# Moving eight rows of each segment from one softmax to the other in a memory-recurrent attention kernel

## The chip, the cores and the metric

One NeuronCore of one Trainium2 chip runs the whole program. The metric is the device time of one execution in microseconds, the median of several runs. The core's engines work side by side: TensorE (PE, its weight loads listed apart as PEld), VectorE (DVE), ScalarE (ACT), GpSimd (POOL) and the queue that starts the DMA transfers (SP). Each engine runs its own instructions in a fixed order and waits on semaphores for the others.

## The reference: what is computed

2048 tokens of width 512 go through two blocks, each with a layer norm ahead and a residual sum. The first is attention with a memory, cut into 64 segments of 32 tokens that run one after the other; the second is a two-layer perceptron (512 to 1792 to 512, gelu).

```python
for s in range(n_seg):                                  # 64 segments
    h = concatenate([mem, xs], axis=1)                  # 8 memory rows + 32 tokens
    q, k, v = (einsum('btd,dhe->bhte', h, W) for W in (Wq, Wk, Wv))   # 32 heads of 128
    scores = einsum('bhqe,bhke->bhqk', q, k) * scale
    scores = where(mask, scores, -1e9)                  # memory rows see all 40 keys, tokens are causal
    o = einsum('bhqk,bhke->bhqe', softmax(scores), v)
    o = einsum('bhte,hed->btd', o, Wo)
    mem = o[:, :8, :]                                   # memory of the next segment
    outs.append(o[:, 8:, :])
```

Only the eight memory rows pass from one segment to the next. The chain from one memory to the next (projection, scores, softmax, product with the values, output projection) is the sequential part; everything else may be done beside it.

## The kernel before, in words

**Three kinds of rows.** A segment's 40 rows are its 8 memory rows, its first 24 tokens and its last 8 tokens, called late here. The first two kinds make 32 rows, which fill a 32-column tile of TensorE's array: `hT` holds them, and the passes `Q0`, `Q1`, `K0`, `K1`, `V0`, `V1` (16 heads each, four units of four 128x32 matmuls with 512 columns) project them with the segment's order of work. The late rows of four segments (a block) make 32 rows too, `hB`; the passes `F0`, `F1` project them a block ahead, keys in the first segment of a block, queries in the second, values in the third. In the fourth, `F` is the output projection of the late rows of the block before (`wo_B`). The results lie in `QTB`, in a region of `KALL` and in `VBD`.

**Two softmaxes.** `sc_mm` makes the scores of the memory rows and the late rows together (parts `SC0`, `SC1`, 16 heads each). For each head the stationary operand `ZC` has 32 columns: the 8 memory queries and the 8 late queries of this head in the place that belongs to the head, zeros elsewhere, so that two heads share one 32-row strip of the result. The moving operand has 64 columns: the 32 keys of the segment (token and memory) and 32 late keys, of which the head's 8 stand in its place. A half therefore has a score tile of 128 rows x 2 slots x 64 columns. `sc_softmax` takes the maximum over both slots (`nmc`), then for each slot an exponential with its sum (`Ea`, `EC`), a reciprocal (`ra`, `rsc`), and a multiply that also separates even from odd strips (`PCa`, `PC`); one 32x32 transpose of all of it gives `PTC`. `pv_c` (`PV0`, `PV1`) multiplies with the values `VS` and, for late keys, with `VBD`; one evacuation goes to the memory columns of `OT` (`OTm`), and after `PV1` `pv_c_b` evacuates the late rows' part to `OTB`. `qb_fill` copies the late queries of the next segment into `ZC` ahead of time, on GpSimd.

`sa_mm` makes the scores of the 24 token rows (part `SA`): 32 matmuls with 32 columns, eight heads a strip, a tile of 128 rows x 8 x 32. In `QT` the eight memory queries still stand in the last columns, so their scores come out too and are not used. `SA`'s softmax and `sa_tail` (multiply `PA`, transpose `PTA`, four copies to the block-diagonal `BD`) run into the next segment, whose part `PVA` (`pv_a`) multiplies with the values; two evacuations go to `OT` (`OTx0`, `OTx1`).

**What sets the order.** TensorE's order is written out by hand in `ORDERS`, one list for each of the four segments of a block; for the third it runs Q and K passes, `SC0`, V and `F1` units, `SC1`, more V and `F1` units, `PV0`, `PVA`, a unit of `F1`, two units of `WO`, `PV1`, six units of `WO`, `SA`, `F0`. (`WO` is the output projection.) The other engines' orders come from a planner, `schedule` at L235: it places each operation, in the order of due times in `PLAN`, into the earliest gap of its engine, with a duration written beside each operation (`dur`). An operation made with `either` may go to one of several engines; the one that ends it first is taken, VectorE with a handicap of 0.2 (`LEAN`). `HOME` fixes some of them: `PA` and the first copy of memory queries `ZCm0` go to GpSimd.

**Instruction blocks.** `align` (L476) counts TensorE's instructions in blocks of 256. At the start of a segment it sets how many spare weight loads (`pad`, emitted in the passes at L869) bring the segment to a fixed place in its block: `PHASE` is 0, 64, 128, 192 for the four kinds of segment. If it is past that place by no more than `SLIP` (24), none are inserted; past that, the spares fill up to the same place of the next block, at most 8 in a unit (`PADS`). `ni` beside each TensorE operation is its count of instructions.

Lines used below: L871 and L604 are the passes, L1036 `sc_mm`, L1044 to L1063 `sc_softmax`, L1074 and L1079 `pv_c`, L1104 `sa_mm`, L1114 to L1118 its softmax, L1125 `PA`, L1127 `PTA`, L1131 `BD`, L1142 `pv_a`, L1170 the output projection, L1176 the new memory (`hT`), L926 the copy of memory queries into `ZC`, L933 `qb_fill`, L912 the transposes of queries and keys, L889 and L890 evacuations, L1364 a matmul of the perceptron that runs early.

Of the kernel before, what the change touches and what calls it, by code (L numbers as in the profile page):

```python
# [28 lines left out]
HALVES = ("kq", "KA", "QT", "ZCm", "VS", "nmc", "Ea", "EC", "ra", "rsc", "PCa", "PC", "PTC", "OTm", "OTx", "KB", "QTB", "VSB")  # L29
# [5 lines left out]
         57: (("w1", 0, 0.6),), 58: (("hn", 3, 0.2), ("w1", 6, 0.4)), 59: (("w1", 1, 0.1), ("w1", 2, 0.8)), 60: (("w1", 3, 0.2), ("w1", 4, 0.5)), 61: (("w1", 5, 0.1),)}  # L35
# [13 lines left out]
        "Ea0": (4.18,) * 4,  # L49
        "EC0": (4.59,) * 4,  # L50
        "ra0": (4.66,) * 4,
        "PCa0": (4.86,) * 4,
# [11 lines left out]
        "Ea1": (5.51,) * 4,  # L64
        "EC1": (5.92,) * 4,
        "ra1": (5.98,) * 4,
        "PCa1": (6.1,) * 4,
# [6 lines left out]
        "OTB": (8.2, 8.48, 8.24, 8.2),  # L74
        "SAp": (7.37,) * 4,
# [13 lines left out]
        "ZCb": (5.92, 3.35, 3.35, 3.35),  # L89
# [13 lines left out]
         ("B", "Q", 0, (0, 5)), "Q0", ("B", "Q", 0, (1, 4)), "Q1", "Z", "SC0", "SC1", ("B", "Q", 1, (0, 5)), "PV0", "PV1", "SA", "WO", ("T", "WO", 0, 3),  # L103
# [35 lines left out]
class Sched:  # L139
# [419 lines left out]
P = 128  # L559
SEG = 32  # L560
MEM = 8
NA = 24
E = 128
# [4 lines left out]
HP = H // 2  # L568
F = 1792
# [52 lines left out]
def build_kernel(nc, A_x, A_mem0, A_Wq, A_Wk, A_Wv, A_Wo, B_w1, B_b1, B_w2, B_b2, out):  # L622
# [3 lines left out]
    with st:  # L626
# [18 lines left out]
        maskR = sb("maskR", [P, 2, 64])  # L645
        maskA = sb("maskA", [P, 32])
        maskCF = sb("maskCF", [P, P], F32)
        maskAF = sb("maskAF", [P, 32], F32)
# [3 lines left out]
        KALL = sb("KALL", [P, 4 * HP + 1, 32, 2])  # L652
        QTB = sb("QTB", [P, 2, HP, 32, 2])
        QT = sb("QT", [P, HP, 32, 2])
        ZC = sb("ZC", [P, 2, H, 32])
# [3 lines left out]
        nmc = sb("nmc", [P, 2, 2], F32)  # L659
        smc = sb("smc", [P, 2, 2], F32)  # L660
        rsc = sb("rsc", [P, 2, 2], F32)
        EC = sb("EC", [P, 2, 2, 64], F32)
        PC = sb("PC", [P, 2, 2, 64, 2])
        PTC = sb("PTC", [P, 2, 2, 64, 2])
        even = sb("even", [P, 2], F32)
        SA = sb("SA", [P, 8, 32], F32)
# [3 lines left out]
        PA = sb("PA", [P, 4, 32, 2])  # L670
        PTA = sb("PTA", [P, 4, 32, 2])
        BD = sb("BD", [P, 2, 4, 4, NA, 2])
# [27 lines left out]
        def sc_place(bank):  # L700

            w = quad[:, bank, 0:128] if bank < 4 else ps[bank][:, 0:128]
            return w.rearrange("p (a n) -> p a n", a=2), ("ps", bank)
# [23 lines left out]
        mL = maskL[:].rearrange("p (a b) -> p a b", a=2)  # L727
        for hl in range(2):
            S.op("pool", lambda e, hl=hl: e.affine_select(mL[:, hl, 8:16], mL[:, hl, 8:16], pattern=[[1, 8]], compare_op=ALU.not_equal, fill=1.0,
                                                          base=8 * hl, channel_multiplier=-1), reads=["maskL"], writes=["maskL"])  # L730
            S.op("pool", lambda e, hl=hl: e.affine_select(mL[:, hl, :], mL[:, hl, :], pattern=[[0, 16]], compare_op=ALU.not_equal, fill=1.0,
                                                          base=-16 - hl, channel_multiplier=1), reads=["maskL"], writes=["maskL"])

        S.op("pool", lambda e: e.memset(maskR[:], 0.0), writes=["maskR"])
        for sl in range(2):
            for i in range(4):
                v = maskR[:, sl, 32 + 8 * i:40 + 8 * i]
                for hl in range(2):
                    if i == 2 * sl + hl:
                        if hl == 0:  # L740

# [647 lines left out]
        for s in range(NS):  # L1389
# [46 lines left out]
            def tail(s):  # L1436
# [15 lines left out]
                if 0 < s < NS - 1:  # L1452
                    qb_fill(s + 1, [S.last_writer[("KA", s % 2, 0)]])
# [233 lines left out]
```

## Time and profile before

| what | value |
|---|---|
| time, median of 3 runs | 819.95 us (818.89 to 820.13) |
| span of the profiled execution | 817.0 us (the profile gives no other time of this execution) |
| TensorE busy | 780.8 us, 96% |
| VectorE, ScalarE, GpSimd busy | 622.1, 529.6, 351.2 us |
| first segment's Q pass to the last segment's `SA` | 31.8 us to 711.3 us of the span |

The 64 segments take most of the span; ahead of them the weights are loaded, behind them the perceptron runs. Three cautions for reading: a matmul's end is modelled and overlaps the next one's start, so distances between starts say more than busy time; a row of the order of time can stand for many instructions in a row (x16); and a wait for several semaphores is put down to one of them.

### The profile page before, as it was taken

What the parts mean: (1) busy time and instruction counts of PE and PEld (TensorE: products, weight loads), DVE (VectorE), ACT (ScalarE), POOL (GpSimd) and SP (SyncE); (2) the same over time, 40 slices, a digit from 0 to 9 for tenths busy, and PEclk for the clock granted to TensorE, in tenths of its full rate; (3) what the DMA queues carried; (4) which work ended last, traced back from release to release, by engine and by line L of the source; (5) the groups of instructions that cost most, each with busy time, mean ns of one, the idle gap of its engine ahead of it and who ended that gap; (6) DMA issues with size and microseconds to landing.
All of it is one profiled execution on the core that took longest, in us unless ns stands there. A gap on an engine that the chain in (4) does not pass through costs nothing.

```text
span 817.0 us, 43604 instructions
## 1 busy us (share of the span) xinstructions
PE 780.8 (96%) x19317; PEld 426.6 (52%) x18878; DVE 622.1 (76%) x2008; ACT 529.6 (65%) x1522; POOL 351.2 (43%) x886
## 2 busy tenths in 40 slices
PE   3788999999999999999999999999999999999998
PEld 1345555555556555555555556555555555544443
DVE  3268797989898989898989898888899887833211
ACT  2446677767776767777777777767676766643442
POOL 5023334545454545454545454545463535367200
PEclk9989999999999999999999999999999999999999
DMA  8950010111101010101010201010112131265200
GB/s 341 391 173 16 4 25 15 30 30 27 32 21 39 17 42 14 45 10 43 10 49 10 49 10 49 10 49 3 49 29 62 37 91 26 76 173 147 55 26 26
DMA packets 65449, 48.03 MB, mean 59 GB/s; under 512 B 29028, under 2 KB 61676, under 8 KB 65260
## 3 DMA queue, kind: packets, MB, share of 16 engines
q1 hardware_dynamic: 64928, 44.98, 18.5%
q8 instruction: 150, 2.46, 1.3%
q14 instruction: 39, 0.32, 0.1%
q10 hardware_dynamic: 332, 0.27, 0.1%
HBM read 31.08 MB, written 8.13 MB: 48 GB/s over the span
## 4 chain that ended last, share of the span: by engine, by line
PE 77%; DVE 8%; ACT 7%; SPq 5%; issue 1%; DMA 1%; DVEq 0%
PE ps L871 33%; PE ps L1170 15%; PE quad L1576 6%; PE ps L604 5%; PE ps L1569 5%; ACT EC L1053 4%; PE quad L1074 4%; ACT kq L889 3%; DVE KALL L912 3%; SPq L791 2%; PE ps L1209 2%; DVE PC L1061 2%; SPq L774 2%; PE ps L1104 2%; DVE nmc L1044 2%; PE quad L1142 2%
## 5 line engine op out<-in xcount | busy, mean ns | idle before, releaser
L871 PE MATMUL ps<-WQ,hT 128*32 128x512 bf16 x2048 | 159.9, 384 | 5.7 <-DVE hT L1176 5.6
L1170 PE MATMUL ps<-WO,OT 128*32 128x256 bf16 x4224 | 141.3, 274 | 1.4 <-DMA WO<-in_A_Wo_dram 0.9
L871 PE MATMUL ps<-WV,hT 128*32 128x512 bf16 x1780 | 142.5, 379 | 0.0
L890 ACT ACTIVATE kq<-ps 128x512 bf16<-128x512 f32 x146 | 87.2, 597 | 66.1 <-PE ps L871 65.8
L1125 POOL TENSOR_TENSOR PA<-SA,rsa 128x256 bf16<-128x256 f32 x64 | 39.8, 621 | 187.4 <-DVE rsa L1118 174.5
L889 ACT CAST kq<-ps 128x512 bf16<-128x512 f32 x160 | 93.4, 583 | 37.8 <-PE ps L871 37.8
L1170 PEld LDWEIGHTS ps<-WO,OT 128*32 128x32 bf16 x4224 | 96.4, 96 | 24.4 <-issue 2.9
L1131 POOL COPY BD<-PTA 32x192 bf16<-32x192 bf16 x256 | 96.4, 376 | 16.7 <-DVE PTA L1127 0.9
L1061 DVE SCALAR_TENSOR_TENSOR PC<-EC,rsc,even 128x128 bf16<-128x128 f32 x256 | 94.6, 371 | 6.6
L871 PE MATMUL ps<-WK,hT 128*32 128x512 bf16 x1292 | 93.6, 379 | 0.0
L871 PEld LDWEIGHTS ps<-WQ,hT 128*32 128x32 bf16 x2048 | 60.5, 96 | 59.8 <-issue 19.4
L912 DVE STREAM_TRANSPOSE KALL<-kq 128x256 f32<-128x256 f32 x160 | 70.5, 441 | 22.9 <-ACT kq L889 20.6
L1053 ACT ACTIVATE EC<-quad,nmc 128x64 f32<-128x64 f32 x252 | 77.1, 311 | 7.6 <-DVE nmc L1044 0.9
L604 PE MATMUL ps<-WK,hT 128*32 128x512 bf16 x756 | 76.5, 382 | 0.0
L889 ACT CAST VS<-ps 128x512 bf16<-128x512 f32 x126 | 73.8, 586 | 0.9
L889 ACT CAST OT<-quad 128x128 bf16<-128x128 f32 (+1 forms) x193 | 65.2, 358 | 10.7 <-PE quad L1079 7.7
L912 DVE STREAM_TRANSPOSE QT<-kq 128x256 f32<-128x256 f32 x128 | 57.0, 446 | 18.7 <-ACT kq L890 18.6
L871 PEld LDWEIGHTS ps<-WV,hT 128*32 128x32 bf16 x1780 | 51.9, 96 | 33.7 <-issue 1.4
L1572 ACT ACTIVATE WQ<-ps,b1t 128x512 bf16<-128x512 f32 x42 | 28.9, 688 | 51.9 <-PE ps L1569 51.9
L1116 ACT ACTIVATE SA<-SA 128x256 f32<-128x256 f32 x64 | 26.7, 417 | 55.0 <-DVE SA L1115 52.7
L871 PEld LDWEIGHTS ps<-WK,hT 128*32 128x32 bf16 x1292 | 38.5, 97 | 44.5 <-issue 19.6
L1222 POOL TENSOR_TENSOR opT<-TTB,TTS 32x64 bf16<-32x64 f32 x128 | 40.3, 315 | 32.4 <-DVE opT L1176 23.2
(160 smaller groups left out, 1485.9 us busy)
## 6 DMA issues: line engine op xcount, KB each, us to landing
WV<-in_A_Wv_dram SPq DMA_DIRECT2D x4, 1024.0 KB, 10.4
WK<-in_A_Wk_dram SPq DMA_DIRECT2D x4, 1024.0 KB, 18.0
WQ<-in_A_Wq_dram SPq DMA_DIRECT2D x4, 1024.0 KB, 18.9
WO<-in_A_Wo_dram SPq DMA_DIRECT2D x16, 256.0 KB, 7.8
v_last<-VSB SPq DMA_DIRECT2D x60, 64.0 KB, 3.1
VBD<-v_last SPq DMA_DIRECT2D x60, 64.0 KB, 2.9
h_mid<-xr SPq DMA_DIRECT2D x16, 128.0 KB, 1.9
WQ<-h_mid SPq DMA_DIRECT2D x4, 512.0 KB, 4.3
```

Of the source, the lines that this page charges most:

```text
L604: return e.add_instruction(mybir.InstMatmult(name="I-%d" % (4000000 + _kept[0]), engine=mybir.EngineType.PE, start_tensor_calc=start, stop ...
L871: ins = e.matmul(o, l, m, start=(k == 0), stop=(k == DC - 1), tile_position=(0, 32 * j), skip_group_check=True)
L889: return {"act": (lambda e: e.copy(out, src), t_act(n, ps_)), "dve": (lambda e: e.tensor_copy(out, src), 0.155 + 1.0e-3 * n * fast)}
L890: return {"act": (lambda e: e.mul(out, src, scale_), t_act(n, ps_)), "dve": (lambda e: e.tensor_scalar(out, src, scale_, None, ALU.mult), ...
L912: S.op("dve", lambda e: e.transpose(out, src), reads=[("kq", i)], writes=[key], dur=t_dve(256) + 0.02)
L1053: return e.activation(EC[:, r, sl, :], o[:, sl, :], ACTF.Exp, bias=nmc[:, r, sl:sl + 1], accum_out=smc[:, r, sl:sl + 1])
L1061: S.op("dve", lambda e, sl=sl, xc=xc: e.scalar_tensor_tensor(PC[:, r, :, :, sl], xc, rsc[:, r, sl:sl + 1], ev, ALU.mult, ALU.mult), reads= ...
L1131: S.narrow(S.op("pool", lambda e, j=j, rows=rows: e.tensor_copy(BD[rows, par, :, j, :, :], PTA[rows, :, 0:NA, :]), reads=["PTA"], writes=[ ...
L1170: ins = e.matmul(ps[bank][32 * j:32 * j + 32, 0:256], lhs(slot(h)), wo_cols(h, b), start=(k == 0), stop=(k == 15), tile_position=(0, 32 * ...
L1222: return e.tensor_tensor(o[32 * q:32 * q + 32, c:c + 2], x, y, ALU.add)
L1569: ins = e.matmul(ps[bank][:, 0:SBT], W1[:, cc, fc * P:(fc + 1) * P], hnT_of(k)[:, cc, :], start=(cc == 0), stop=(cc == DC - 1))
L1576: S.op("pe", lambda e: e.matmul(quad[:, t, :], gT_of(k, fc)[:, t * P:(t + 1) * P], W2[:, fc, :], start=(fc == 0), stop=(fc == FC - 1)), re ...
```

## The change

The late queries and the late keys leave the memory rows' softmax and join the token rows'.

- `ZC` holds memory queries alone. Four heads (before: two) share a 32-row strip, so a half has one slot of 64 columns: one maximum, one exponential, one reciprocal, one multiply, a transpose of half the size. `ZC` has one buffer instead of two; `qb_fill` goes. Matmuls of `sc_mm` keep their number and size.
- In `QT`, once the memory queries have been copied out, `ql_fill` puts the segment's 8 late queries in their place; `kl_fill` puts the 8 late keys behind the segment's 32 keys in `KALL`, whose rows become 40 wide. Both may go to ACT, VectorE or GpSimd, and both stand ahead of `SA`. `sa_mm`'s 32 matmuls have 40 columns instead of 32, the softmax 8x40 columns instead of 8x32.
- `sa_tail` gets a second multiply (`PL`, 64 columns, VectorE or GpSimd) ahead of the transpose, which is 160 words wide instead of 128, and a masked copy `BDL` of the late keys' probabilities (VectorE or GpSimd). `BD` keeps all 32 rows' columns.
- `pv_c` has 16 instead of 32 columns in its eight matmuls, 64 instead of 128 in its two. `pv_a` has 64 instead of 48 columns in its sixteen, and four more with 64 columns for the late keys. `OTB` is evacuated after `PVA`, a segment later.
- The masks are rebuilt to match, planner durations and due times are set anew, and one early load of the perceptron's weights moves a segment later.

```diff
-        "Ea0": (4.18,) * 4,
-        "ra0": (4.66,) * 4,
-        "PCa0": (4.86,) * 4,
+        "QL": (7.0,) * 4,
+        "KL": (6.5,) * 4,
+        "PL": (12.86,) * 4,
+        "BDL": (15.6,) * 4,
...
-        return HOP[p.eng]
+        return HOP[p.eng] + (0.06 if o.eng == "pe" else 0.0)
...
+        def ql_fill(s):
+            bk, sg = s // 4, s % 4
+            dst, src = words(QT[:])[:, :, NA:SEG], words(QTB[:, bk % 2])[:, :, 8 * sg:8 * sg + 8]
+            S.either({"act": (lambda e: e.copy(dst, src), 0.34), "dve": (lambda e: e.tensor_copy(dst, src), 0.24), "pool": (lambda e: e.tensor_copy(dst, src), 0.34)},
+                     reads=[("QTB", bk % 2, q) for q in range(2)], writes=[("QL", 0), ("QT", 0), ("QT", 1)])
+
+        def kl_fill(s):
+            bk, sg = s // 4, s % 4
+            dst, src = k_words(s % 2)[:, :, 32:LK], k_words(bk % 2, True)[:, :, 8 * sg:8 * sg + 8]
...
                     for j in range(4):
                         h = 16 * r + 4 * j + i
...
-                        sl = i // 2
-                        ins = e.matmul(o[32 * j:32 * j + 32, sl, :], ZC[:, par, h, :], rhs, start=False, stop=(i == 3),
+                        ins = e.matmul(o[32 * j:32 * j + 32, :], zc_window(h), rhs, start=False, stop=(i == 3),
                                        tile_position=(0, 32 * j), skip_group_check=True)
...
         def sc_softmax(s, r, bank):
-            for sl, names in enumerate((("Ea", "sa", "ra", "PCa"), ("EC", "smc", "rsc", "PC"))):
+            S.op("act", lambda e: e.activation(EC[:, r, :], o, ACTF.Exp, bias=nmc[:, r:r + 1], accum_out=smc[:, r:r + 1]),
+            S.op("dve", lambda e: e.reciprocal(rsc[:, r:r + 1], smc[:, r:r + 1]), reads=[("smc", r)], writes=[("rsc", r)], dur=0.16)
+            S.op("dve", lambda e: e.scalar_tensor_tensor(PC[:, r].rearrange("p k b -> p b k"), xc, rsc[:, r:r + 1], ev, ALU.mult, ALU.mult),
...
         def sa_tail(s):
+            S.either({k: ((lambda e: e.tensor_tensor(PA[:, 4].rearrange("p (i u) r -> p r i u", i=4), SA[:, :, SEG:LK].rearrange("p (r i) u -> p r i u", r=2), bcl, ALU.mult)), w)
+                      for k, w in (("dve", 0.24), ("pool", 0.32))}, ["SA", "rsa"], ["PL"], after=after)
...
-                S.narrow(S.op("pool", lambda e, j=j, rows=rows: e.tensor_copy(BD[rows, par, :, j, :, :], PTA[rows, :, 0:NA, :]), ...
+                S.narrow(S.op("pool", lambda e, j=j, rows=rows: e.tensor_copy(words(BD[rows, par, :, j, :, :]), words(PTA[rows, 0:4])), ...
+            S.either({k: ((lambda e: e.tensor_tensor(BDL[:, par], src, msk, ALU.mult)), w) for k, w in (("dve", 0.3), ("pool", 0.45))},
+                     reads=["PTA", "maskD"], writes=[("BDL", par)])
...
         def pv_a(s):
+                for r in range(2):
+                    for t in range(2):
+                        rows = slice(64 * t, 64 * t + 64)
+                        o = quad[:, 2 + t, 256 * r:256 * r + 256].rearrange("p (n q) -> p n q", q=32)[:, :, NA:SEG]
+                        ins = e.matmul(o, VBD[rows, bk % 2, sg, r, :], BDL[rows, s % 2, r], start=False, stop=True, tile_position=(64 * t, 0), skip_group_check=True)
-                 writes=AQ, dur=0.29, mode=MH, ni=32)
+                 writes=AQ, dur=0.27, mode=MH, ni=40)
...
                 elif name == "SA":
+                    ql_fill(s)
+                    kl_fill(s)
                     sa_mm(s, bank_of[name])
```

More of the change, by code (lines that the diff above doesn't have):

```diff
@@ L28 @@
 PAUSES, PAUSE_IN, PAUSE_US = 3, 64, 0.5
[L29 removed]
+HALVES = ("kq", "KA", "QT", "ZCm", "VS", "nmc", "EC", "rsc", "PC", "PTC", "OTm", "OTx", "KB", "QTB", "VSB")
 BONUS = {}
@@ L562 @@
 NA = 24
+LK = 40
 E = 128
@@ L1145, in pv_a @@
-            S.op("pe", f, reads=[("VS", par, 0), ("VS", par, 1)] + [("BD", s % 2, j) for j in range(4)], writes=AQ, dur=0.29, mode=MH, ni=32)
+                        c0 = 256 * (k // 4) + 32 * (k % 4)
+                        o = quad[:, 2 + t, c0:c0 + 160].rearrange("p (b q) -> p b q", q=32)[:, 0:5:4]
+                        e.matmul(o, VS[rows, par, k // 4, (k % 4) * E:(k % 4 + 1) * E], BD[rows, s % 2, k // 2, 2 * t:2 * t + 2, :, k % 2],
+                                 start=(k == 0), stop=False, tile_position=(64 * t, 0), skip_group_check=True)
```

246 lines of the change are left out of this document (110 added, 136 removed).

## The prediction, made before the change was built

> **What bounds the kernel now.** I read the page first, then busy time by stretch, then the order of time of one steady segment, TensorE first and the engines that feed it after.
>
> ```profile
> span 817.0 us, 43604 instructions
> PE 780.8 (96%) x19317; PEld 426.6 (52%) x18878; DVE 622.1 (76%) x2008; ACT 529.6 (65%) x1522; POOL 351.2 (43%) x886
> ```
>
> ```profile
> 376.24:387.31 11.07, 10.40 (x296) 5.76 (x284) 9.33 (x32) 7.42 (x22) 5.42 (x13) 1.00 0.02 3
> 387.31:397.73 10.42, 10.37 (x296) 5.82 (x277) 9.00 (x31) 7.73 (x24) 4.79 (x13) 1.00 0.06 17
> 397.73:408.04 10.31, 10.28 (x297) 5.73 (x285) 9.66 (x33) 7.50 (x22) 5.66 (x15) 1.00 0.02 5
> 408.04:418.35 10.31, 10.28 (x297) 5.71 (x286) 9.10 (x31) 7.51 (x23) 4.47 (x12) 1.00 0.37 93
> ```
>
> These are four consecutive segments (one block) at full clock: TensorE is the only engine without room, so the loop is worth what TensorE's start times say. A busy PE can still wait, since a matmul's 0.40 us tail covers short gaps; I therefore read distances between starts, here in the third segment.
>
> ```profile
> 401.19 0.30 PE L1036 MATMUL quad<-KALL,ZC 128*32 128x64 bf16 x16
> ...
> 403.19 0.61 PE L871 MATMUL ps<-WV,hT 128*32 128x512 bf16 x8
> 403.62 0.40 PE L871 MATMUL ps<-WV,hB 128*32 128x512 bf16 x4
> 404.05 0.27 PE L1074 MATMUL quad<-PTC,VS 64*128 64x32 bf16 x8
> 404.14 0.23 PE L1079 MATMUL quad<-PTC,VBD 64*128 64x128 bf16 x2
> 404.20 0.37 PE L1142 MATMUL quad<-BD,VS 64*128 64x48 bf16 x16
> 404.51 0.40 PE L871 MATMUL ps<-WV,hB 128*32 128x512 bf16 x4
> 404.73 0.62 PE L1170 MATMUL ps<-WO,OT 128*32 128x256 bf16 x16
> 405.29 0.27 PE L1074 MATMUL quad<-PTC,VS 64*128 64x32 bf16 x8
> 405.40 0.22 PE L1079 MATMUL quad<-PTC,VBD 64*128 64x128 bf16 x2
> 405.55 1.50 PE L1170 MATMUL ps<-WO,OT 128*32 128x256 bf16 x48
> ```
>
> Eight matmuls of 512 columns take 0.43 (403.19 to 403.62), so four take 0.215. The four at 403.62 hold the engine until 403.835, yet the first PV of the memory rows (PV0) starts at 404.05: 0.215 lost. What it waits for is in VectorE's order:
>
> ```profile
> 402.56 0.39 DVE L1061 SCALAR_TENSOR_TENSOR PC<-EC,rsc,even 128x128 bf16<-128x128 f32 x1
> 402.86 0.15 DVE L1058 RECIPROCAL rsc<-smc 128x1 f32<-128x1 f32 x1
> 402.99 0.29 DVE L1044 TENSOR_REDUCE nmc<-quad 128x2 f32<-128x128 f32 x1
> 403.20 0.35 DVE L1061 SCALAR_TENSOR_TENSOR PC<-EC,rsc,even 128x128 bf16<-128x128 f32 x1
> 403.59 0.31 DVE L1063 STREAM_TRANSPOSE PTC<-PC 128x128 f32<-128x128 f32 x1
> ```
>
> PTC lands at 403.90 and PV0 starts 0.15 later. Not all of the 0.215 is that wait, because the array changes its tiling there (128x32 to 64x128). A late segment shows the change alone:
>
> ```profile
> 686.54 0.39 PE L1364 MATMUL ps<-xr,hT 128*128 128x512 bf16 x1
> 686.87 0.27 PE L1074 MATMUL quad<-PTC,VS 64*128 64x32 bf16 x8
> ```
> ```profile
> 686.19 0.31 DVE L1063 STREAM_TRANSPOSE PTC<-PC 128x128 f32<-128x128 f32 x1
> ```
>
> There PTC was ready at 686.50, and from one 512-column matmul (0.215) to PV0 still 0.33 pass: the change costs 0.33 - 0.215 = 0.115. So the removable wait at PV0 is about 0.10 to 0.11 a segment. At PV1, 0.56 from the start of 16 matmuls whose work is 0.44 (48 take 1.32, below in the same order as at 405.55) leaves 0.12, the change alone.
>
> **The change part by part.** *Memory softmax.* Each half loses one exponential with its accumulator read, one reciprocal and one L1061 multiply, and its transpose and maximum halve. Before PV0 the second multiply (403.20) and the interposed second reciprocal go. From 402.56 the chain is one multiply (0.39) and a transpose below 0.31, so PTC is ready near 403.3 instead of 403.90. That is before 403.835, and the wait is gone: 58 steady segments x 0.11 = **-6.4 us**. Bounds: 0 if the wait is all tiling change, -7 if all 0.12 beyond it go.
>
> In the three first looping segments no late-token pass fills TensorE, and the same chain stands bare:
>
> ```profile
> 78.43 0.83 PE L871 MATMUL ps<-WV,hT 128*32 128x512 bf16 x12
> 79.73 0.27 PE L1074 MATMUL quad<-PTC,VS 64*128 64x32 bf16 x8 [0.46 <-ACT EC L1053]
> ```
>
> 12 matmuls take 0.645 and the tiling change 0.115, so 1.30 - 0.76 = 0.54 is wait. The chain shortens by about 0.6, so I take 0.5 x 3 = **-1.5 us** (0 to -1.6). The first segment's gain is lost: its output projection waits for weights. In the segments after 680 the hT wait follows, PV0 has none.
>
> *PV matmuls.* PV0 and PV1 keep their count at half the columns. Two of 128 columns took 0.06 (404.14 to 404.20), so with 64 about 0.03: -0.03 each. PVA gains four matmuls and its 16 go from 48 to 64 columns. The row's eight 32-column ones took 0.09 to 0.11, 0.0125 each, which I read as a load bound; 16 in 0.31 less the tiling change are 0.0125 each as well, with 48 columns. 64 columns stream in the time of half of 128, so they fit nearly. Four more cost 0.05. Net -0.06 + 0.05 + 0.02 = 0.01, x 61 = **+0.6 us** (0 to +4).
>
> By the Trainium skill, "TensorE: Matmul & The Clock Gate", section Back-to-back issue gap, matmuls of 1 to 64 columns all cost about the 25 ns issue floor. It agrees that the wider 16 cost nothing; at its price the four would be 0.1 us, the term +3.7 and the time 3.1 us later. The rows' 0.0125 (two row groups side by side) decide.
>
> *Token softmax, 256 to 320 columns.*
>
> ```profile
> L1044 DVE TENSOR_REDUCE nmc<-quad 128x2 f32<-128x128 f32 x126 | 36.8, 292 | 0.6 <-PE quad L1036 0.6
> L1114 DVE TENSOR_REDUCE nma<-ps 128x8 f32<-128x256 f32 x64 | 27.2, 425 | 2.9 <-PE ps L1104 0.9
> L1222 POOL TENSOR_TENSOR opT<-TTB,TTS 32x64 bf16<-32x64 f32 x128 | 40.3, 315 | 32.4 <-DVE opT L1176 23.2
> ```
>
> 128 more elements cost 0.133, so 64 cost 0.067 on each of three VectorE steps; the exponential gets about 0.035. The probabilities PA start 0.235 later. The new small multiply (PL, 64 elements) is near 0.3 on GpSimd by the last row, or 0.2 on VectorE. Behind PA on GpSimd stands the copy of the memory queries (ZC) that the scores SC0 need:
>
> ```profile
> 399.98 0.62 POOL L1125 TENSOR_TENSOR PA<-SA,rsa 128x256 bf16<-128x256 f32 x1 [2.57 <-DVE rsa L1118]
> 400.62 0.29 POOL L926 COPY ZC<-QT 128x128 bf16<-128x128 bf16 x1
> ```
> ```profile
> 389.29 0.62 POOL L1125 TENSOR_TENSOR PA<-SA,rsa 128x256 bf16<-128x256 f32 x1 [2.29 <-DVE rsa L1118]
> 390.19 0.29 POOL L926 COPY ZC<-QT 128x128 bf16<-128x128 bf16 x1 [0.28 <-DVE QT L912]
> ```
>
> In the third segment the copy follows PA at once; in the second it has 0.28 to spare. SC0 starts at 401.19, the copy ends at 400.91: with 0.15 for the signal (as at PV0) the slack is 0.13. So PA alone pushes SC0 by 0.235 - 0.13 = 0.1 in segments like the third, by nothing in those like the second; PL adds up to 0.3 where it is queued on GpSimd ahead of the copy, and little on VectorE, in the gap before QT. From 0 to 0.33 a segment; I take 0.05, near the second segment's slack: 58 x 0.05 = **+2.9 us** (0 to +19).
>
> *Cover.* The copies of late queries and keys into QT and KALL may run any time from the memory queries' copy (400.91) to the output projection's end (near 407.0), behind which the token scores SA stand; ACT (7.5 of 10.3) and GpSimd (5.7) have room. If put in VectorE's queue ahead of KALL they would cost TensorE their 0.3. The masked copy BDL needs only PTA (401.2) and is wanted at PVA; late it would cost up to its 0.3. OTB's evacuation goes to after PVA, the same size. The wait of the next Q for hT stays: its chain and its filling work do not change. The masks' fewer GpSimd steps lie under the weight load.
>
> *Instruction stream.* PVA adds four matmuls and four weight loads to each segment. The kernel fills segments up to a fixed place in 256-instruction blocks with spare weight loads (L869):
>
> ```profile
> L869 PEld LDWEIGHTS <-hT x16: 92/92/93, 376.2 to 418.3; 128*32 128x32 bf16 x16
> ```
> ```profile
> 385.66 0.24 PE L1104 MATMUL ps<-KALL,QT 128*32 128x32 bf16 x12
> 386.54 0.30 PE L1104 MATMUL ps<-KALL,QT 128*32 128x32 bf16 x20 [0.64 <-issue]
> ```
> ```profile
> q8 instruction: 150, 2.46, 1.3%
> ```
>
> Four spares a segment exist, eight instructions come: each segment overruns by about four. By the code, after some six segments (slip over 24) about 230 spares are inserted, some ten times. A block is one packet (38,195 TensorE instructions / 150 = 255), and where it comes late, the token scores stand for 0.64, as here in a first segment of a block. I take +1.0 us (0: the spares ride under matmuls; +9: 0.3 in 16 first segments and 0.4 at ten refills).
>
> The Trainium skill, "Runtime: NRT & Kernel Launch", section Instruction fetch mechanics, has 16 KiB blocks fetched ahead, the crossing mostly hidden; by it the term is 0 and the time 1.0 us earlier. The row with 0.64 shows a crossing that is not.
>
> **The sum.** -6.4 - 1.5 + 0.6 + 2.9 + 1.0 = -3.4 us. The profile gives the span, 817.0; the median of 819.95 lies 2.95 above, which I leave as it is around the span: 819.95 - 3.4 = **816.5 us**.
>
> **Rivals.**
> *The copy behind PA (slower).* One mechanism at one place: GpSimd takes PL ahead of ZC in every second segment kind or more, SC0 starts 0.33 late there. For it: PA already ends where ZC begins in the third segment, and VectorE is the fuller engine (9.66 against 5.66). Against: VectorE has a gap before QT in the other kinds. It decides once SC0's mean delay passes 0.14 (8 us over 58). With half the segments at 0.33 the term is 9.6 + 1.5 for the rest, in place of 2.9: 816.5 + 8.2 = 824.7.
> *Fetch eats it.* At its upper end the fetch term is 9, in the middle 4.5: 816.5 + 3.5 = 820.0. For it the 0.64; against, that the same code ran 10.31 in segments that cross blocks too.
> *The wait was the tiling change.* Then it does not do what it says in steady state: 819.95 - 1.5 + 0.6 + 1.0 = 820.0. Against: 686.87.
> *More than that.* SC0 is not delayed, and the first segments' stalls (11.07 against 10.31) shrink as blocks move: 816.5 - 2.9 - 2.5 = 811.
>
> **Chances.** Forecast (813.5 to 819.5) 0.45; slower rival 0.22; fetch 0.15; tiling change 0.06; more 0.12. Under 0.2%, 1.64 us, nothing can be told from no change. Faster (below 818.3): 0.36 + 0.12 + 0.04 = 0.52. Within: 0.09 + 0.08 + 0.05 = 0.22. Slower: 0.26. The range, leaving half of "more" and some of the slower rival out, is 811 to 824.5.
>
> **What would show it.** Right: PV0 starts 0.33 after the last four-matmul unit in steady segments, PTC ends 0.4 or more ahead, SC0 follows K1 at 0.22 a unit, and 58 segments near 10.25. Wrong: a SC0 that starts more than 0.1 after K1 with ZC just before it on GpSimd; starts of SA with long "issue" waits, and L869 in the hundreds at every sixth segment; or PV0 still 0.43 after its unit with PTC early.

## The result and the profile after

| kernel | median | against the kernel before in the same runs |
|---|---|---|
| before | 819.42 us (817.12 to 820.13) | |
| changed | 840.11 us (838.66 to 842.28) | 1.0254 (95% interval 1.0229 to 1.0279) |

The change costs 20.7 us where 3.4 us were forecast as gain. The profiled execution took 838.79 us, 1.8 us more than its span. The ratios in this document leave out executions far above the fastest of their kernel, of which there was one, 1978 us in experiment 11, whose median counts it. Three rows of the page of the changed kernel answer to those of before: total busy time, and the queue that brings TensorE's instructions (packets, MB, share).

```profile
span 837.0 us, 47057 instructions
PE 785.2 (94%) x19573; PEld 452.1 (54%) x22165; DVE 608.8 (73%) x1868; ACT 519.7 (62%) x1379; POOL 305.7 (37%) x832
q8 instruction: 164, 2.69, 1.4%
```

The memory softmax did get shorter (VectorE 622.1 to 608.8, ScalarE 529.6 to 519.7, GpSimd 351.2 to 305.7 us), yet TensorE has 3287 more weight loads (18,878 before), and 14 more instruction packets. The change itself adds 4 x 64 = 256 of them. The others are spares, by the view of their line in each kernel. Its last line is the busy share over 40 slices of the span, in tenths. After:

```profile
L857 PEld LDWEIGHTS <-hT x3096: 92/97/158, 50.0 to 723.1; 128*32 128x32 bf16 x194
L857 PEld LDWEIGHTS <-hB x520: 92/97/97, 127.4 to 655.9; 128*32 128x32 bf16 x174
...
busy tenths in 40 slices 0045055360909090909090909090905639300000
```

and the same line before:

```profile
busy tenths in 40 slices 0045300000000000000000000000000005200000
```

A slice is 20.9 us, two segments: 9, 0, 9, 0 says that some 230 spares (the code sets 232) pass in one segment of every four, where the kernel before had four or none in a segment. The stretches of four consecutive segments of the changed kernel, one block (columns as in the prediction's), show what that does:

```profile
295.73:307.36 11.63, 10.62 (x301) 7.24 (x504) 9.02 (x29) 7.13 (x20) 4.99 (x13) 1.00 0.02 4
307.36:317.73 10.37, 10.37 (x300) 5.86 (x277) 8.84 (x29) 7.52 (x21) 4.25 (x13) 1.00 0.06 18
317.73:327.96 10.23, 10.23 (x300) 5.95 (x280) 9.08 (x30) 7.72 (x21) 5.29 (x15) 1.00 0.02 4
327.96:339.04 11.08, 10.36 (x300) 5.80 (x292) 9.97 (x31) 7.18 (x20) 3.29 (x10) 1.00 0.35 86
```

The first segment has 504 weight loads and takes 11.63 us; the third, without spares, 10.23, below the 10.31 of before. Over segments 4 to 59 the four kinds take 11.81, 10.42, 10.28 and 10.94 us on average, from the first Q matmul to the next one's; before 10.70, 10.42, 10.36 and 10.33. So the loss sits in the segment that is filled, and in the one ahead of it. TensorE's order of time in the first of these segments:

```profile
301.65 0.40 PE L859 MATMUL ps<-WV,hT 128*32 128x512 bf16 x4
301.99 0.18 PE L1063 MATMUL quad<-PTC,VS 64*128 64x16 bf16 x1
302.54 0.24 PE L1063 MATMUL quad<-PTC,VS 64*128 64x16 bf16 x7 [0.38 <-issue]
...
305.71 0.22 PE L1089 MATMUL ps<-KALL,QT 128*32 128x40 bf16 x8
306.56 0.33 PE L1089 MATMUL ps<-KALL,QT 128*32 128x40 bf16 x24 [0.63 <-issue]
```

PV0 starts on time, 0.34 after its unit, issues one matmul and then stands although nothing that it waits for is late ("issue"); the token scores SA do the same, exactly 256 instructions later. The traffic of this very stretch, in 40 slices of 0.29 us, holds nothing but instruction packets:

```profile
GB/s 0 56 0 0 0 0 0 0 0 0 0 0 0 0 0 56 0 0 0 0 0 0 0 0 0 0 0 56 0 0 0 0 0 0 0 0 0 0 0 0
DMA packets 3, 0.05 MB, mean 4 GB/s; under 512 B 0, under 2 KB 0, under 8 KB 0
```

The second packet lies in the slice from 300.1 to 300.4, the third in 303.6 to 303.9. Each of the two standstills ends 2.1 to 3.0 us after the start of a packet: the instructions came late.

One further stall appears once, at the end of segment 55. Four blocks of 128 rows of the perceptron's input are brought in early, in segments 53 to 57: a DMA from `h_mid` to `xT`, a normalization on VectorE (L1352, L1348 before), a transposing DMA. VectorE's order in the changed kernel:

```profile
643.67 0.41 DVE L1352 TENSOR_SCALAR xn<-xT,agg,rst 128x512 bf16<-128x512 bf16 x1 [5.51 <-DMA xT<-h_mid]
644.00 0.44 DVE L1186 STREAM_TRANSPOSE TT<-ps 128x256 f32<-128x256 f32 x1
644.48 0.39 DVE L1180 TENSOR_TENSOR hT<-TT 64x32 bf16<-64x32 f32 x2
```

VectorE stands 5.51 us for that transfer, and the new memory hT is queued behind it. SP's queue says why the transfer is late, first after, then before:

```profile
636.45 3.22 SPq L990 DMA_DIRECT2D VBD<-v_last  x4
639.71 0.43 SPq L1351 DMA_DIRECT2D xT<-h_mid  x1
```
```profile
621.41 0.37 SPq L1347 DMA_DIRECT2D xT<-h_mid  x1
622.25 2.33 SPq L989 DMA_DIRECT2D VBD<-v_last  x4
```

Before, the load stood ahead of the four transfers of late values; after, behind them, since the planner had put the normalization of the row block before it later on VectorE (5.56 us into segment 55, before 1.99), and `xT` came free later. TensorE's order shows the cost, and the stretch after it the granted clock (the number behind the fifth engine):

```profile
640.24 0.83 PE L1213 MATMUL ps<-WO,OTB 128*32 128x512 bf16 x12 [0.25 <-PE ps L1089]
644.96 0.41 PE L859 MATMUL ps<-WQ,hT 128*32 128x512 bf16 x4 [3.89 <-DVE hT L1180]
```
```profile
645.20:648.40 3.20, 3.20 (x40) 1.84 (x103) 2.21 (x7) 1.07 (x2) 0.62 (x1) 0.55 0.00 0
```

Segment 55 takes 14.67 us, and segment 56 begins at a clock of 0.55 and takes 12.68.

### The profile page after: what moved, and what is told of

Its sections match the earlier page's. It is cut to its first block, busy times and chain, and to the rows that moved or that the text cites. A ratio compares the mean times of both kernels' runs of the same rounds, so it can differ in the third digit from the quotient of the medians.

```text
span 837.0 us, 47057 instructions
## 1 busy us (share of the span) xinstructions
PE 785.2 (94%) x19573; PEld 452.1 (54%) x22165; DVE 608.8 (73%) x1868; ACT 519.7 (62%) x1379; POOL 305.7 (37%) x832
## 4 chain that ended last, share of the span: by engine, by line
PE 90%; SPq 5%; issue 3%; DMA 1%; DVE 1%; DVEq 0%
PE ps L859 43%; PE ps L1174 15%; PE ps L603 7%; PE quad L1575 6%; PE ps L1568 4%; PE ps L1213 4%; PE quad L1063 3%; SPq L779 2%; SPq L762 2%; PE quad L1035 2%; PE ps L1089 2%; PE quad L1135 2%; PE ps L1368 2%; DMA WO<-in_A_Wo_dram 1%; PE quad L1067 1%
## 5 line engine op out<-in xcount | busy, mean ns | idle before, releaser
L878 ACT ACTIVATE kq<-ps 128x512 bf16<-128x512 f32 x160 | 95.6, 598 | 47.9 <-PE ps L859 47.6
L1174 PEld LDWEIGHTS ps<-WO,OT 128*32 128x32 bf16 x4224 | 100.9, 96 | 19.4 <-issue 4.3
L877 ACT CAST OT<-quad 128x128 bf16<-128x128 f32 (+1 forms) x183 | 57.5, 341 | 53.9 <-PE quad L1067 51.6
L1120 POOL COPY BD<-PTA 32x128 f32<-32x128 f32 x256 | 74.1, 290 | 41.2 <-DVE PTA L1116 27.9
L859 PEld LDWEIGHTS ps<-WQ,hT 128*32 128x32 bf16 x2048 | 57.6, 95 | 58.0 <-issue 23.5
L857 PEld LDWEIGHTS <-hT 128*32 128x32 bf16 x3096 | 52.0, 97 | 35.4 <-DVE hT L1180 9.8
L859 PEld LDWEIGHTS ps<-WV,hT 128*32 128x32 bf16 x1780 | 54.2, 96 | 26.8 <-issue 2.2
L1186 DVE STREAM_TRANSPOSE TT<-ps 128x256 f32<-128x256 f32 x66 | 29.7, 450 | 46.4 <-PE ps L1174 46.3
L859 PEld LDWEIGHTS ps<-WK,hT 128*32 128x32 bf16 x1292 | 37.8, 96 | 34.7 <-issue 15.4
L1102 ACT ACTIVATE SA<-SA 128x320 f32<-128x320 f32 x64 | 30.1, 471 | 39.6 <-DVE SA L1101 39.4
L1050 DVE SCALAR_TENSOR_TENSOR PC<-EC,rsc,even 128x128 bf16<-128x128 f32 x128 | 51.3, 401 | 4.5
```

What stands on the lines that cost most here:

```text
L857: e.ldweights(l, tile_position=(0, 32 * j))
L859: ins = e.matmul(o, l, m, start=(k == 0), stop=(k == DC - 1), tile_position=(0, 32 * j), skip_group_check=True)
L877: return {"act": (lambda e: e.copy(out, src), t_act(n, ps_)), "dve": (lambda e: e.tensor_copy(out, src), 0.155 + 1.0e-3 * n * fast)}
L878: return {"act": (lambda e: e.mul(out, src, scale_), t_act(n, ps_)), "dve": (lambda e: e.tensor_scalar(out, src, scale_, None, ALU.mult), ...
L1050: S.op("dve", lambda e: e.scalar_tensor_tensor(PC[:, r].rearrange("p k b -> p b k"), xc, rsc[:, r:r + 1], ev, ALU.mult, ALU.mult), reads=[ ...
L1120: S.narrow(S.op("pool", lambda e, j=j, rows=rows: e.tensor_copy(words(BD[rows, par, :, j, :, :]), words(PTA[rows, 0:4])), reads=["PTA"], w ...
```

## The experiments

**1. No spares at all.** The blocks then move by 24 instructions against each block of four segments.

```diff
-PHASE = (0, 64, 128, 192)
+PHASE = ()
```

> The changed kernel without any spare weight loads (the phase table is empty), so that the blocks of 256 instructions move by 24 against the segments of each block of four. Refill theory (the 224 to 232 spares before every fourth segment make the instruction stream come late at PV0 and SA, 1.1 to 1.8 us a time, 14 times): the segments of 11.8 go, all run at 10.25 to 10.6, total 815 to 822. Rival theory (the token rows' longer softmax, PL and the eight new instructions themselves slow the loop): 836 to 842 as before this edit, since all of that work stays. Third possibility, that the spares do pay for themselves: without them the place of the block changes costs 0.3 to 0.6 in every segment, 835 to 850.

818.09 us (812.99 to 822.48), 0.9987 of before (0.9961 to 1.0013). In one line 22 us are back, with all of the moved work still there, so that work isn't slow; and leaving the place of the blocks to chance costs no 0.3 to 0.6 a segment, though some segments still lose up to 1.1 us (11.34 and 11.25 are the longest). The stall at the end of segment 55 shrank to 0.78, since the transfers fell in another order: the function `windows` of the planner sets transfers by the ends of the instruction blocks, which this edit moves. That is part of the 22, and this run alone does not tell the two parts apart.

**2. The kernel before, with spares.**

```diff
                 if owed > FETCH_N - SLIP:
                     owed = 0
+                owed += FETCH_N * (seg % 4 == 0 and 4 < seg < 60)
```

> The kernel before the change with 256 more spare weight loads in every first segment of a block from segment 8 to 56 (13 times), which leaves each segment at the same place in the 256-instruction blocks; nothing else differs. Refill theory: first segments grow from 10.7 to about 11.8 and the segments before them by 0.3 to 0.6, so 13 x 1.1 to 1.7: 834 to 842. Rival theory (spares ride under the matmuls, the loss of the change lies in its own work): 819 to 821.

834.68 us, 1.0199 of before (1.0177 to 1.022): 15.4 us for 13 refills, 1.2 each, with nothing of the change in it. TensorE's order in one such first segment (12.30 us long) stands at PVA and at SA with the same wait:

```profile
303.58 0.23 PE L1143 MATMUL quad<-BD,VS 64*128 64x48 bf16 x5
304.37 0.32 PE L1143 MATMUL quad<-BD,VS 64*128 64x48 bf16 x11 [0.56 <-issue]
...
307.25 0.37 PE L1105 MATMUL ps<-KALL,QT 128*32 128x32 bf16 x26
308.21 0.22 PE L1105 MATMUL ps<-KALL,QT 128*32 128x32 bf16 x6 [0.59 <-issue]
```

The spares alone make the loss. The rival (they ride under the matmuls) falls. One part of the expectation failed: over segments 4 to 59 the filled kind is 15.3 us longer in all, but the segments ahead of it only 0.4 us in all, not 0.3 to 0.6 each.

**3. Without the four late matmuls.** `pv_a` loses its second loop, so that the late keys' values do not enter the token rows' result; eight instructions a segment go with it.

```diff
-                for r in range(2):
-                    for t in range(2):
...
-                        ins = e.matmul(o, VBD[rows, bk % 2, sg, r, :], BDL[rows, s % 2, r], start=False, stop=True, tile_position=(64 * t, 0), skip_group_check=True)
```

> The changed kernel without the four matmuls that add the late keys' values to the token rows' PV (their contribution is left out of the result; softmax, PL, BDL and all copies stay). A segment then has eight TensorE instructions fewer, 574 to 578, and two or three spares a segment suffice. Refill theory: 810 to 816 (undisturbed segments of 10.22 to 10.28, PV0 0.33 after its unit). Rival theory (longer token softmax and PL ahead of the copy ZC delay SC0 and SA): 835 to 840, since these stay. It does not tell the four matmuls' own time (0.05 x 61 = 3 us by estimate) from the refills; the first run does.

812.71 us, 0.9934 (0.9903 to 0.9965), as the refill theory has it; segments from 4 to 59 run 10.18 to 10.55, but for 12.24 in segment 55. The price of the four matmuls can be read from its PVA:

```profile
274.46 0.40 PE L1135 MATMUL quad<-BD,VS 64*128 64x64 bf16 x16
274.78 0.40 PE L859 MATMUL ps<-WV,hB 128*32 128x512 bf16 x4
```

Sixteen matmuls of 64 columns and the change of tiling take 0.32; with the four late ones it is 0.38 (below). So four cost 0.06.

**4. Eight loads saved in the value passes.** In each of the four lists of `ORDERS`, the third one shown:

```diff
-('V0', 0, 1), ('V1', 0, 1), ('V0', 1, 4), ('F1', 0, 1), ('SC1', 0, 99), ('V1', 1, 2), ('F1', 1, 2), ('V1', 2, 4),
+('V0', 0, 1), ('V1', 0, 2), ('V0', 1, 3), ('V1', 2, 3), ('V0', 3, 4), ('SC1', 0, 99), ('F1', 0, 2), ('V1', 3, 4),
```

> The whole change, with the order of the value passes altered so that two more units a segment use the weights of the unit before them (V0 c0, V1 c0, V1 c1, V0 c1, V0 c2, V1 c2, V0 c3, then SC1): eight weight loads fewer a segment, so that segments are 574 to 578 instructions and three spares a segment suffice, as in the kernel before. SC1 stands one unit (0.215 us) later; it has about 0.5 to spare before PV1. Refill theory: 811 to 817. Rival theory (the change's own work is slow): 835 to 842. If SC1's place costs something, PV1 is late by up to 0.2 in 58 segments: 820 to 826.

818.86 us, 0.9993 (0.998 to 1.0006). The refills are gone (about three spares a segment) and the time comes back to that of before, but not below it as expected: third and fourth segments run 10.33 to 10.36 where the changed kernel's undisturbed ones ran 10.22, and segments 55 and 56 stall (12.56 and 12.41). The guess of a late PV1 was wrong: PV1 starts 7.5 us into the segment as in the changed kernel. What makes the next Q start 0.1 later was not settled.

**5 to 8. Loads saved where no unit ends later; the early load; the spares spread.** Run 5 shares loads between Q and K, run 6 adds a later release of the last early load (and an earlier one of the transposing DMA that follows the load before it), run 7 has only this edit of `EARLY`, run 8 only another placing of the spares.

```diff
# runs 5 and 6, in each list of ORDERS
-('Q0', 2, 3), ('Q1', 0, 1), ('Q0', 3, 4), ('K0', 2, 4), ('Q1', 1, 4),
+('Q0', 2, 3), ('K0', 2, 3), ('Q0', 3, 4), ('K0', 3, 4), ('Q1', 0, 4),
# runs 6 and 7, in EARLY
-56: (("hx", 3, 0.3), ("hn", 2, 0.7)),
+56: (("hn", 2, 0.3), ("hx", 3, 0.9)),
# run 8
-FETCH_AT, PADS, SLIP = 65, 8, 24
-PHASE = (0, 64, 128, 192)
+FETCH_AT, PADS, SLIP = 65, 3, 24
+PHASE = (0, 128, 0, 128)
```

> The whole change, with eight weight loads a segment saved where no unit ends later: Q0 and K0 take the third and fourth part of the hidden width in turn, so that K0's units use the weights that Q0 just loaded (before: Q0 c2, Q1 c0, Q0 c3, K0 c2, K0 c3, Q1; now: Q0 c2, K0 c2, Q0 c3, K0 c3, Q1). Segments are 574 to 578 instructions with 4 to 7 spares. Refill theory: no refills, first segments 10.4 to 10.6 in place of 11.8, others 10.20 to 10.35, but the stall ahead of segment 56 (VectorE waits for a load of the early perceptron rows before it makes hT) stays with 2 to 7 us: 812 to 818. If the change's own work costs what the first experiments left open (the four matmuls, 0.05 x 61), it is at the upper end. Rival theory (the moved work is slow by itself): above 820.

> As the run before it, and the last early load of perceptron rows (h_mid to xT, row block 3) is released a segment later, so that its VectorE step no longer stands ahead of the memory's hT at the end of segment 55. If that wait is the cause of the long segment 55 (14.67 in the changed kernel, 12.2 to 12.6 in two other runs) and of the slow start of segment 56, both go back to 10.3 to 10.6: 2 to 4 us below the run before it, 809 to 814. Rival: the stall comes from the DMA itself and moves with it to segment 56: no difference.

> The changed kernel with the spare weight loads as they were (224 to 232 in every first segment) and only the last early load of perceptron rows released a segment later. If the stall in segments 55 and 56 is worth what its trace showed (4.2 us of standstill and about 1.3 more in segment 56 beyond a refill): 834 to 836. If the refills hide it or the stall moves: 839 to 841.

> The changed kernel with the same number of instructions in a block of four segments (10 x 256), but the spares spread over all four segments, 56 to 59 in each, at most 3 a unit, in place of 230 in the first. If what costs is that 815 instructions pass in one segment, 90 a microsecond at the passes in place of 40 to 55, no place comes late and the time is 812 to 822. If each additional block of 256 costs its 1.1 to 1.7 us wherever it stands, it stays at 836 to 842.

| run | median | against before |
|---|---|---|
| 5, shared loads of Q and K | 821.42 us | 1.0032 (1.0015 to 1.0048) |
| 6, the same and the early load later | 815.92 us | 0.996 (0.9943 to 0.9976) |
| 7, the early load later, spares as they were | 833.45 us | 1.0176 (1.0161 to 1.0191) |
| 8, spares spread | 828.51 us | 1.0115 (1.0102 to 1.0128) |

Run 5 is 3 us above its expectation; its segments 55 and 56 take 14.88 and 12.96. Run 6 ends that stall (10.26 and 10.53), 5.5 us below run 5, and run 7 is 6.7 us below the changed kernel, so the early load cost about 6. Run 6 holds all of the moved work and is 0.4% faster than the kernel before. Four consecutive segments of it:

```profile
331.09:341.53 10.44, 10.44 (x301) 5.51 (x277) 8.79 (x29) 7.13 (x20) 4.93 (x13) 1.00 0.02 5
341.53:351.88 10.35, 10.35 (x300) 5.67 (x276) 9.03 (x29) 7.63 (x21) 4.24 (x14) 1.00 0.05 16
351.88:362.16 10.28, 10.28 (x300) 5.72 (x281) 9.13 (x30) 7.73 (x21) 5.33 (x15) 1.00 0.01 3
362.16:372.43 10.27, 10.27 (x301) 5.44 (x280) 9.17 (x30) 7.18 (x20) 3.29 (x10) 1.00 0.38 93
```

From run 7 to run 6 only the spares and eight loads a segment go: 17.5 us, 1.25 for each of 14 refills. This is a net figure. By the two traces, over segments 4 to 59, the first segments become 16.7 us shorter in all (1.3 for each of the 13 refills among them, 1.2 in the second run) and the fourth 4.7 us, but the second ones 4.1 us longer, for which see runs 9 and 10. Run 8 has as many spares as the changed kernel and lies between: with the stall of its segments 55 and 56 (14.44 and 13.37, some 7 us above 10.4 each) taken off, spread spares cost about 828.5 - 7 - 815.9 = 6 us, a third of the bunched ones. By this count density decides most of it, though the edit also moves the places where the blocks end; the expected 812 to 822 was missed because that stall was left out of the expectation, and because a further block of 256 costs 0.4 (6 us by 14) even where it is spread.

**9 and 10. The place of the blocks.** Run 6 with `PHASE` moved by four and by eight.

```diff
-PHASE = (0, 64, 128, 192)
+PHASE = (4, 68, 132, 196)      # run 9; (8, 72, 136, 200) in run 10
```

> The sixth run's kernel (shared loads for Q and K, the last early load later) with the phase table moved by four instructions (4, 68, 132, 196), so that the blocks of 256 end at the same instruction of the output projection and of the token scores as in the kernel before. In the sixth run seven second segments of a block stood for 0.65 to 1.2 us at the 451st instruction, inside the output projection. If the place of the block's end decides, these go: 811 to 814. If four instructions are too few to matter: 815 to 817 as in the sixth run.

> As the ninth run with the table moved by eight (8, 72, 136, 200). If the place decides smoothly: 810 to 814, and the first segments (10.4 to 10.5, block's end in the token scores) move by a tenth; if not, 814 to 818.

816.79 us, 0.9958 (0.9942 to 0.9973), and 816.88 us, 0.9963 (0.9951 to 0.9975): no difference to run 6. In each of the three, six of the 14 second segments from 5 to 57 still lose 0.6 to 1.2 us inside the output projection. In run 6, segment 53:

```profile
600.44 1.04 PE L1174 MATMUL ps<-WO,OT 128*32 128x256 bf16 x31
602.41 0.60 PE L1174 MATMUL ps<-WO,OT 128*32 128x256 bf16 x13 [0.93 <-issue]
```

The stall follows the block's end (it stands four instructions earlier in the segment in run 9), so it is a late block; but the same place stalls in some second segments and not in others. Where it stalls, the packet starts 6.7 to 7.2 us into the segment, elsewhere 5.8 to 6.6. These stalls come with run 5's order of the passes and not with the moved work: runs 5, 6, 9, 10 and 12 have six of them each (run 12 is the kernel before with that order) and run 11 two; the kernel before and runs 2, 3, 4 and 8 have none in these segments, the changed kernel and run 7 one. What lets a packet start late stays open.

**11. PL always behind PA on GpSimd.** Run 9 with one choice taken away.

```diff
-                      for k, w in (("dve", 0.24), ("pool", 0.32))}, ["SA", "rsa"], ["PL"], after=after)
+                      for k, w in (("pool", 0.32),)}, ["SA", "rsa"], ["PL"], after=after)
```

> The ninth run's kernel with the small multiply PL always on GpSimd, behind PA and ahead of the copy ZC (64 times in place of 15). This is the slower rival of the prediction taken by itself: there, ZC 0.3 late delays SC0 by up to 0.33 in each of 49 more segments, up to 16 us over the ninth run, 5 to 8 at the slack of 0.13 to 0.28. If SC0 has room (in the changed kernel's trace it follows K1 in every steady segment), the time is the ninth run's within 2 us.

816.48 us, 0.9947 (0.9926 to 0.9968): no difference to run 9. The group of the multiply, and then GpSimd and TensorE in one third segment, show why:

```profile
L1114 POOL TENSOR_TENSOR PA<-SA,rsa 128x64 bf16<-128x64 f32 x64 | 19.2, 301 | 0.0
```
```profile
315.27 0.30 POOL L1114 TENSOR_TENSOR PA<-SA,rsa 128x64 bf16<-128x64 f32 x1
315.51 0.29 POOL L923 COPY ZC<-QT 128x128 bf16<-128x128 bf16 x1
```
```profile
315.16 0.84 PE L859 MATMUL ps<-WK,hT 128*32 128x512 bf16 x12
315.85 0.30 PE L1035 MATMUL quad<-KALL,ZC 128*32 128x64 bf16 x16
```

All 64 multiplies stand ahead of the copy, which ends at 315.80, and the scores SC0 start 0.05 later, 0.69 after the three units ahead of them in place of 0.64. So the rival's mechanism exists, but it delays SC0 by 0.05 to 0.06 in the first, third and fourth segments and by nothing in the second (medians against run 9), not by 0.33. That is 2.4 us over segments 4 to 59 at most, and the total does not show it. The groups' column of idle time misses it (0.0 ahead of the scores), since the tail of the matmuls before covers it.

**12. The kernel before with run 5's order.** The same edit of `ORDERS` as in run 5.

> The kernel before the change with the same shared loads of Q and K (eight loads a segment fewer, 12 to 16 spares fill the place). Control for the winner: if the shared loads are worth nothing by themselves, 819 to 820, and what the changed kernel gains against it is the change's own; if they gain by themselves (Q1 starts later, behind the token scores' read of its bank), 815 to 818.

834.42 us, 1.0185 (1.016 to 1.0209): neither. Six second segments stall in the output projection as in run 6 (4.5 us of "issue" waits). The new order also made the planner evacuate `kq` on VectorE 49 times, and in many segments the multiply ahead of PV0 takes 0.53 where it took 0.35, beside GpSimd's copies of `BD` (mean of all multiplies 402 ns, before 371). It is no control for run 6: whether the shared loads gain by themselves stays open. It does show what the prediction's first term rests on. In one such segment, VectorE and TensorE:

```profile
282.35 0.53 DVE L1061 SCALAR_TENSOR_TENSOR PC<-EC,rsc,even 128x128 bf16<-128x128 f32 x1
282.92 0.31 DVE L1063 STREAM_TRANSPOSE PTC<-PC 128x128 f32<-128x128 f32 x1
```
```profile
282.75 0.41 PE L871 MATMUL ps<-WV,hB 128*32 128x512 bf16 x4
283.38 0.27 PE L1074 MATMUL quad<-PTC,VS 64*128 64x32 bf16 x8 [0.22 <-DVE rsc L1058]
```

PTC lands at 283.23 and PV0 starts 0.15 later, 0.63 after its unit in place of 0.43: 0.2 more on VectorE is 0.2 more for TensorE. In the kernel before, this chain had no slack.

## Why the prediction was wrong, step by step

**Memory softmax, -6.4: right.** TensorE in an undisturbed third segment of the changed kernel:

```profile
323.62 0.40 PE L859 MATMUL ps<-WV,hB 128*32 128x512 bf16 x4
323.95 0.26 PE L1063 MATMUL quad<-PTC,VS 64*128 64x16 bf16 x8
324.07 0.19 PE L1067 MATMUL quad<-PTC,VBD 64*128 64x64 bf16 x2
324.10 0.40 PE L1135 MATMUL quad<-BD,VS 64*128 64x64 bf16 x16
324.33 0.22 PE L1141 MATMUL quad<-BDL,VBD 64*128 64x64 bf16 x4
324.48 0.40 PE L859 MATMUL ps<-WV,hB 128*32 128x512 bf16 x4
```
```profile
323.14 0.23 DVE L1052 STREAM_TRANSPOSE PTC<-PC 128x64 f32<-128x64 f32 x1
```

PV0 starts 0.33 after its unit (forecast 0.33, before 0.43), and PTC ends at 323.37, 0.58 ahead of it (forecast 0.4 or more). What is left is the change of tiling, 0.115. That is 0.10 a segment, 5.8 us over 58.

**First segments, -1.5: right.** In segments 1 to 3 PV0 starts 0.77 after the first of the 12 matmuls ahead of it, in place of 1.30 (forecast 0.76). These segments take 10.79, 9.78 and 9.95 in place of 11.92, 10.38 and 10.50. The further 0.6 in segment 1 is not shown to belong to the change: in run 2, whose instructions are those of the kernel before up to segment 7, it takes 10.97.

**PV matmuls, +0.6: too small, within its bounds.** PVA's rise from 0.31 to 0.38 is what was worked out (0.05 and 0.02), and the four late matmuls at 0.06 come near the rate of 0.0125 a matmul. But fewer columns saved less than the 0.03 a half of the estimate: by the medians of segments 4 to 59 PV0 to PVA falls from 0.16 to 0.14, and PV1 to the output projection from 0.26 to 0.23. So about 0.04 a segment remains, +2.4 over 61. By the Trainium skill, "TensorE: Matmul & The Clock Gate", section Back-to-back issue gap, the four would cost 0.1 by estimate, at about 25 ns each; the 0.06 of this case does not agree with that floor.

**Token softmax, +2.9: too large, and the slower rival falls.** The multiply PL ran 50 times on VectorE (236 ns) and 14 times on GpSimd (299 ns), within the prices given. In the changed kernel's second to fourth segments SC0 starts 3.45 to 3.46 us into the segment, as before, so the term is 0. Two sizes were off. In the third segments PA starts 0.12 later and not 0.235 (in the fourth it is 0.27, where GpSimd had stood idle for 0.14 between PA and the copy). And the slack was taken as 0.28 less 0.15 for the signal, a figure from VectorE to PV0; run 11 shows SC0 0.05 after GpSimd's copy, so the slack was 0.23. With PL behind PA in every segment it is used up, and SC0 moves by 0.05 (run 11).

**Instruction stream, +1.0 within 0 to 9: this step failed.** The place was right (spares in the hundreds, "issue" at the starts of SA), and three things in it were wrong.
- *How often.* By the code's own count the four segments without spares have 583, 582, 582 and 581 instructions, six more than the 576 of their place on average and not four. Two readings were short: the view with x16 spares reaches to 418.3 and holds the next block's first four, so that a block had 12; and each segment got on average a ninth instruction, a wait on a semaphore (four more a block by the code's count). So a block is 36 - 12 = 24 over. That is the whole of `SLIP`, and at 24 the code already fills (the description of the kernel lets 24 pass), so it is filled up every four segments (14 times) and not every sixth (ten).
- *How much.* A refill costs 1.2 to 1.25 us net (runs 2, 6 and 7), since it makes two or three blocks late, at PV0, at SA and in the changed kernel at SA of the segment ahead. The prediction priced one late start at 0.3 to 0.4, from a kernel in which a block of 256 passes in 3.5 to 5.7 us (ten blocks from segment 21 on). In the changed kernel's filled segment 24, two blocks pass in 3.2 each and, in the segment ahead of the next refill, one in 3.1; all three end in a stall.
- *What hides it.* "The spares ride under matmuls" is nearly true of their own time (PV0 starts 6.27 us into a filled segment, 6.21 into the others), and no answer to when the next instructions arrive.

14 x 1.25 = 17.5 in place of 1.0. The rival "Fetch eats it" had this mechanism and put it at 4.5 to 9.

**A step that was not there: the early load, +6 to +7.** The prediction looked at VectorE's and GpSimd's queues for each moved operation and left out SP's: no moved operation issues a transfer, but every time that the planner works with changed, and one load changed places with four others. Runs 6 and 7 price it at 5.5 and 6.7.

Together: 840.1 - 6.7 - 17.5 = 815.9, run 6, 3.4 us below the kernel before (the two terms are differences of these same runs, so the sum is no further test). That the forecast too was -3.4 is partly luck. By the traces, run 6 gains 3.0 us in segments 0 to 3, and from 4 to 59 another 3.0 in the first, 0.9 in the third and 0.9 in the fourth segments of the blocks (0.06 in each third and fourth one, the 0.10 at PV0 less the 0.04 of the PV matmuls). It loses 4.7 in the second ones, whose stalls the forecast did not have. What its eight saved loads do apart from that has no clean control.

## What to carry to other kernels

Count an edit's instructions against every threshold in the code that counts them, and work out exactly when it trips: nine instructions more in 576 cost more than the 0.1 us wait that the change removed, and the ninth, one wait a segment, decided when the threshold was reached. A stretch that is dense in cheap instructions must be priced by when the next block of instructions arrives, not by what the instructions hide under; and filler belongs where it is spread, or nowhere. Where a planner writes the queues, compare the order of each queue before and after, the DMA queue too, also for work that the edit does not touch.

## What the runs showed of the hardware

**Instructions arrive some 2.5 us after their packet starts.** In the changed kernel each of the 123 blocks of 256 instructions between segments 5 and 55 has one instruction packet, which starts 0.1 to 2.1 us after the block's first instruction. No block ends less than 2.2 us after that start, and where the next block is late, the standstill ends 2.2 to 3.0 us after it. So a block that passes in less than its packet's delay plus some 2.2 us ends in a wait: of 36 blocks whose instructions take less than 3.25 us, 28 end in a standstill of more than 0.4 us, of the other 87 one. By the Trainium skill, "Runtime: NRT & Kernel Launch", section Instruction fetch mechanics, instructions come in blocks of 256 and crossing into one is mostly hidden. The size agrees with this case; "hidden" holds for 86 of those 87 blocks and not for 28 of the 36 shorter ones. It is no matter of length alone: before the change a block of 3.9 us stood for 0.64 (at 386.54 in the prediction's view), its packet having started 1.75 us after its first instruction.

**A short standstill can halve the clock, or not.** After the 4.3 us between starts in segment 55 (3.89 by the profile) the granted clock was 0.55 for 3.2 us (above). In run 4 TensorE waited 2.1 us by the profile and 2.46 between starts; the stretch that follows:

```profile
627.20:630.40 3.20, 3.20 (x40) 1.27 (x32) 2.33 (x6) 1.38 (x3) 0.65 (x2) 0.52 0.00 0
```

In run 3 it was 1.94 and 2.30, and the clock stayed at 1.00:

```profile
620.00:622.00 2.00, 1.63 (x32) 0.71 (x31) 1.92 (x6) 0.47 (x1) 0.00 (x0) 1.00 0.00 0
```

The Trainium skill, "TensorE: Matmul & The Clock Gate", section What's actually happening, has a half clock after an idle window of about 3.4 us. The 4.3 agrees; run 4's 2.46 does not by that length alone. In runs 8 and 5 standstills of 4.1 and 4.9 us were followed by a clock of 0.50 over windows of 6.8 us that began while TensorE stood; segment 56 took 13.37 and 12.96 us there. In these runs a standstill of 2.46 us or more thus cost more than its length: an estimate from the granted clock is 1.6 us more in the changed kernel and in run 4 (half of 3.2 us), and some 2.5 to 2.9 us in runs 5 and 8 (half of the 5.0 and 5.7 us that TensorE ran in those windows).
